# Gated linear attention with a feed-forward: the scaled keys of units 9 to 19 put in token order by VectorE block transposes instead of TensorE transposes

## The chip, the cores and the metric

The kernel runs on one core of one Trainium2 chip, as one launch. The metric is the device time of that launch in microseconds (us): 530.71 us before, the median of three runs (530.29 to 530.88). A core has a matrix engine (TensorE; PE in the profile, with its weight loads listed apart as PEld), a vector engine (VectorE; DVE), a scalar engine (ScalarE; ACT), GpSimd (POOL) and a queue that only issues DMAs (SyncE; SP). Each engine takes its instructions strictly in the order in which they stand in its program and waits on semaphores for the others.

## What is computed

For each of 4 x 8 (batch, head) pairs a 48 x 48 state runs over 768 tokens, decayed row by row by `alpha`; the result `y`, laid out as 3072 tokens of 384 values, goes through a feed-forward network of width 2048 with a leaky ReLU. All in float32.

```python
for t in range(S):                       # S = 768, D = 48
    state = alpha[:, :, t, :, None] * state + einsum('bhd,bhe->bhde', k[:, :, t], v[:, :, t])
    y[:, :, t] = einsum('bhd,bhde->bhe', q[:, :, t], state)
x = y.transpose(0, 2, 1, 3).reshape(B * S, H * D)
h = x @ w_in                             # (3072, 384) @ (384, 2048)
out = maximum(0.01 * h, h) @ w_out
```

## The kernel before

**Units.** The attention is cut into 24 units, `u` = 0 to 23: 6 blocks of 128 tokens times 4 batches, all 8 heads in a unit, two heads stacked on 112 of the 128 partitions (48 rows, a gap of 16, 48 rows) and four such pairs side by side. Units 0 to 19 also carry the state on; the last four (`units[u][0] == NC - 1`) do not. Per unit, `attention` (L455) goes through these steps, with a `yield` behind each:

- `scans` (L308): the decay in feature order, `e`, by a VectorE transpose (from unit 9 on) or by TensorE transposes (before), then cumulative products `pc` and reversed sums `rc`.
- `scaled_q`, `scaled_k` (L334, L342): q times `pc` gives `qs`, k times `rc` gives `ks`, both in feature order. From unit 9 on their transposes are those of L289 on VectorE, out of the loads' buffers.
- `scores` (L350): 8 matmuls of `ks` with `qs`; `mask_scores` (L359) copies and masks them to `sm`.
- `k_tokens` (L375): the scaled keys back in token order. Four TensorE transposes of `ks` into a PSUM bank (L380) and a ScalarE copy into `ktok` (L382).
- `outputs` (L385): `y` from state, queries and masked scores (L395, L401), and `kv` from `ktok` and the values (L412), then `y` into `x` (L418, L419). `next_state` (L421) updates the state.

**Feed-forward.** Three units make a block of 384 tokens, `i` = 0 to 7; its x rows are completed by two small DMAs from SBUF to SBUF (`gather`, L442). For each of 16 slices `f` of the width, `ffn_in` (L484) runs 9 matmuls into `ph` (L493: high and low parts of the weights and of x), then on ScalarE `t` = 0.01 ph (L496), on VectorE `t` = max (L499), on ScalarE `gh` (L501), on VectorE `gl` (L505). `ffn_out` (L510) runs 9 matmuls with `gh` and `gl` into the output banks (L520), three items later (`LAG`). There are two `ph` banks, so the matmuls of item n + 2 need the `t` of item n to be done.

**Stages.** Units 0 to 8 run first. Then blocks 0 and 1 run interleaved, while the weights of the next slices are converted (`converting`, L226: raw words to a high part `hi` and a low part, six VectorE steps up to L265 and two of ScalarE). The first two items of that stage are emitted within the attention of units 7 and 8, by the table `STARTS` (L551), behind the `kt` transposes of L380. From block 2 on, the attention steps of units 9 to 23 are emitted between the items: two steps per item in block 2, one and a half later, eight steps a unit.

**Order.** The code is emitted in this order, and a scheduler then sets the order on each engine when the program is built; `issue_after` (`behind`, L108) holds an instruction behind another. SP issues all loads in its own order, and a load into a used buffer waits there until the buffer's last reader is done.

**Buffers.** q, k and alpha have two load buffers each, and a third one for units 0 to 8; `load_next(u, i)` issues the next load into the buffer that unit u gives up.

Of the kernel before, what the change touches and what calls it, by code (L numbers as in the profile page):

```python
# [22 lines left out]
def gated_linear_attn_ffn(ctx, tc, q, k, v, alpha, w_in, w_out, out):  # L23
    nc = tc.nc
# [3 lines left out]
    P = 128  # L28
    C = 128
    NC = S // C  # L30
    NP = H // 2
# [7 lines left out]
    units = [(t, b) for t in range(NC) for b in range(B)]  # L39
# [18 lines left out]
    AHEAD = 3 * UPB  # L58
# [8 lines left out]
    def bank(tag=None):  # L67
        if tag is None:
            tag = kinds[0]
            kinds.append(kinds.pop(0))  # L70
        return ps_x.tile([P, 512], F32, name=tag)
# [36 lines left out]
    def behind(*key):  # L108

        return tc.issue_after(made[key].ins) if key in made else nullcontext()  # L110

    def places(u, i):
        return loads_sb[i] + [spare[i]] if u < AHEAD else loads_sb[i]

    def loaded(u, i):
        return places(u, i)[u % len(places(u, i))]

    def load_next(u, i):

        for n in range(u + 1, u + 4):  # L120
            if n < NU and n - len(places(n, i)) == u:
                load(n, i)
# [4 lines left out]
    def load(u, i):  # L127
        if u >= NU:
            return
        if u >= AHEAD and later is not None:  # L130
            later.append((load, u, i))
            return
        tb, b = units[u]
        ts = slice(tb * C, (tb + 1) * C)
        t, src = loaded(u, i), (alpha, q, k)[i]
        if u < AHEAD:
            n = H if u or i else H // 2
            for h in range(0, H, n):
                nc.sync.dma_start(
                    by_token(t)[:, h:h + n, 0:D], src[b, h:h + n, ts, :].rearrange("h t d -> t h d")  # L140
                )
            return

        for a in range(4):
            off = 32 * (a % 2)
            nc.sync.dma_start(
                t[32 * a:32 * (a + 1), :].rearrange("j (p r) -> j p r", p=NP)[:, :, 0:RUN - off],
                src[b, a // 2::2, ts, :].rearrange("p (j t) d -> j p (t d)", t=T4)[:, :, off:],
            )

    def load_values(u):
        if u >= NU:
            return
        if u >= AHEAD and later is not None:
            later.append((load_values, u))
            return
        tb, b = units[u]
        made["v", u] = nc.sync.dma_start(
            vals_sb[u % NV].rearrange("t (h d) -> t h d", h=H),
            v[b, :, tb * C:(tb + 1) * C, :].rearrange("h t d -> t h d"),  # L160
        )
# [109 lines left out]
    def banks4():  # L271
        return bank().rearrange("r (p n) -> r p n", p=NP)

    def transposed(u, i, name, **kw):

        src = loaded(u, i)
        if u < AHEAD:
            ps = banks4()
            for p in range(NP):
                last = nc.tensor.transpose(  # L280
                    ps[:, p, :], by_token(src)[:, 2 * p:2 * p + 2, :].rearrange("t h d -> t (h d)"), ident
                )
                if u == 0 and p % 2:
                    with tc.issue_after(last.ins):
                        keep_warm(2)
            return ps
        t = atp.tile([P, NP, C], F32, name=name, **kw)
        src = src.rearrange("r (p n) -> r p n", p=NP)[:, :, 0:RUN]
        nc.vector.transpose(  # L289
            t.rearrange("r p (j t) -> r p t j", t=T4),  # L290
            src.rearrange("r p (t d) -> r p t d", t=T4)[:, :, :, 0:32],
        )
        return t
# [4 lines left out]
    live, masked, sums, dense = {}, {}, {}, {}  # L298
# [35 lines left out]
    def scaled_q(u):  # L334
        pc = live[u][0]
        qT = transposed(u, 1, "qs")
        load_next(u, 1)
        qs = qT if u >= AHEAD else atp.tile([P, NP, C], F32, name="qs")
        nc.vector.tensor_tensor(qs, qT, pc, ALU.mult)
        live[u].append(qs)  # L340
# [9 lines left out]
    def scores(u):  # L350

        pe, qs, ks = live[u]
        ss = [banks4(), banks4()]
        for p in range(NP):
            for s, lo in ((0, 0), (1, HB)):
                nc.tensor.matmul(ss[s][:, p, :], ks[lo:lo + D, p, :], qs[lo:lo + D, p, :], start=True, stop=True)  # L356
        live[u].append(ss)

    def mask_scores(u):  # L359
        ss = live[u].pop()  # L360
        sm = [atp.tile([P, NP, C], F32, name="sm", bufs=3) for _ in (0, 1)]
        for s in (0, 1):
            if s and u >= AHEAD:
                nc.vector.tensor_tensor(sm[s], ss[s], mask.unsqueeze(1).broadcast_to([P, NP, C]), ALU.mult)
                continue
            made["sm", u] = nc.scalar.copy(sm[s], ss[s])  # L366
            made["mask", u] = nc.gpsimd.affine_select(  # L367
                out=sm[s], in_=sm[s], compare_op=ALU.is_ge, fill=0.0, base=0, pattern=[[0, NP], [1, C]], channel_multiplier=-1
            )
        masked[u] = sm  # L370
        with behind("mask", u):
            while scalings:
                nc.gpsimd.tensor_tensor(*scalings.pop(0))  # L373

    def k_tokens(u):  # L375
        if units[u][0] < NC - 1:
            ks = live[u][2]
            kt = bank()
            for p in range(NP):
                made["kt", u] = nc.tensor.transpose(kt[:, p * BR:(p + 1) * BR], ks[0:BR, p, :], ident[0:BR, 0:BR])  # L380
            ktok = atp.tile([P, NP, BR], F32, name="ktok", bufs=1)
            made["sm", u] = nc.scalar.copy(ktok.rearrange("t p d -> t (p d)"), kt[:, 0:NP * BR])  # L382
            live[u][2] = ktok

    def outputs(u):  # L385
        tb, b = units[u]
        i, j = divmod(u, UPB)
        pe, qs, ktok = live[u][:3]
        V, W = vals_sb[u % NV], state[b]
        at = i % 3 * (NG + 1)  # L390
        y = banks4()

        if tb:
            for p in range(NP):
                nc.tensor.matmul(  # L395
                    y[0:BR, p, :], W[0:BR, p, :], qs[0:BR, p, :], start=p == 0, stop=False, skip_group_check=True
                )
        for p in range(NP):
            for s, lo, m in ((0, 0, D if tb else HB), (1, HB, D)):
                c = (2 * p + s) * D  # L400
                nc.tensor.matmul(  # L401
                    y[lo:lo + m, p, :], V[:, c:c + m], masked[u][s][:, p, :],
                    start=not tb and p == 0, stop=p == NP - 1, skip_group_check=True,
                )
        del masked[u]
        kv = None
        if tb < NC - 1:
            kv = bank()[:, 0:NP * D].rearrange("d (p e) -> d p e", p=NP)
            for p in range(NP):
                for s, lo, m in ((0, 0, HB), (1, HB, D)):  # L410
                    h = 2 * p + s
                    made["kv", u] = nc.tensor.matmul(  # L412
                        kv[lo:lo + m, p, :], ktok[:, p, lo:lo + m], V[:, h * D:(h + 1) * D], start=True, stop=True
                    )
        load_values(u + NV)
        live[u] = pe, kv
        xh, xl = (x_sb[0:BR, at:at + NP, n, j * C:(j + 1) * C] for n in (0, 1))
        made["xh", u] = nc.scalar.copy(xh, y[0:BR])  # L418
        made["x", u] = nc.vector.tensor_tensor(xl, y[0:BR], xh.bitcast(F32), ALU.subtract)  # L419
# [35 lines left out]
    def attention(first, last):  # L455

        for u in range(first - 1, last):
            new, old = u + 1 < last, u >= first
            if new:
                scans(u + 1)  # L460
                yield
            if old:
                scores(u)
                yield
                mask_scores(u)
                yield
                k_tokens(u)
                sum_up(u)
                yield
            if new:  # L470
                scaled_q(u + 1)
                yield
                scaled_k(u + 1)
                yield
            if old:
                outputs(u)
                yield
                next_state(u)
                if u % UPB == UPB - 1:
                    gather(u // UPB)  # L480
                    ready.add(u // UPB)
                yield
# [71 lines left out]
    for n, _ in enumerate(st):  # L554
# [7 lines left out]
        u = AHEAD - EARLY + converted  # L562
# [13 lines left out]
    new = coming = None  # L576
    for n in range(len(items) + LAG):
        slices = 0
        if n < len(items):
# [17 lines left out]
            elif i == 0:  # L597
# [3 lines left out]
                old, new, coming = new or iter(()), coming, converting(f + SOON + 1, True)  # L601
# [144 lines left out]
```

## Time and profile before

The profiled execution is one run of its own; its span is what the page's shares and all moments below refer to. It and the median of the timed runs are the same within 0.2 us.

| | before |
|---|---|
| time, median of 3 runs | 530.71 us (530.29 to 530.88) |
| span of the profiled execution | 530.9 us |
| instructions | 9962 |
| mean granted TensorE clock | 0.994 |
| ScalarE busy | 230.7 us (43%) |
| GpSimd busy | 62.6 us (12%) |
| units 0 to 8 | about 0 to 66 us |
| blocks 0 and 1, with the conversion of the weights | about 60 to 164 us |
| blocks 2 to 7, with units 9 to 23 until about 450 us | about 163 to 530 us |

The page's groups are one line each: source line, engine, operation, tile written and tiles read, shape, count, then busy time, mean duration, and the idle time of the engine just ahead of them with what ended it. `a` and `b` are PSUM banks, `small` is the tensor that holds the load buffers, the state and the mask, `large` holds x.

### The profile page before, as it was taken

How to read it: one execution, taken by the hardware profiler on the slowest of the kernel's cores; microseconds unless marked ns; L12 is line 12 of the kernel's file. 1: busy time of each engine (PE TensorE's matmuls, PEld its weight loads, DVE VectorE, ACT ScalarE, POOL GpSimd, SP SyncE). 2: the span in 40 equal slices, each digit the busy share in tenths (PEclk: the TensorE clock that was granted, in tenths of full speed). 3: DMA queues.
4: the chain of work that ended last, by engine and by line, in shares of the span. 5: the costliest groups of instructions: out<-in, count | busy, mean ns of one | idle time of the engine just before them, and what ended most of it. 6: DMA issues, size and time to landing. Idle time of an engine off the chain costs nothing.

```text
span 530.9 us, 9962 instructions
## 1 busy us (share of the span) xinstructions
PE 518.5 (98%) x3778; PEld 500.0 (94%) x3778; DVE 379.0 (71%) x695; ACT 230.7 (43%) x489; POOL 62.6 (12%) x143
## 2 busy tenths in 40 slices
PE   8997999999999999999999999999999999999995
PEld 7886999999999999999999999999999999999995
DVE  6998899999999997777577586585786534333331
ACT  2764855555534444444334444345344444333331
POOL 4554500000000111100101101101010000000000
PEclk9998999999999999999999999999999999999998
DMA  9999975545726533552251431433201000101001
GB/s 144 168 175 170 229 172 133 131 122 141 170 45 184 127 84 81 102 134 49 60 111 30 112 83 44 92 74 86 54 15 25 31 16 1 23 1 44 1 0 51
DMA packets 92982, 46.64 MB, mean 88 GB/s; under 512 B 57856, under 2 KB 90112, under 8 KB 92928
## 3 DMA queue, kind: packets, MB, share of 16 engines
q1 hardware_dynamic: 92928, 45.93, 39.5%
q8 instruction: 32, 0.52, 0.4%
q14 instruction: 22, 0.18, 0.1%
HBM read 38.83 MB, written 4.72 MB: 82 GB/s over the span
## 4 chain that ended last, share of the span: by engine, by line
PE 87%; DVE 7%; DMA 4%; issue 1%; SPq 0%; DVEq 0%; ACT 0%
PE ph L493 35%; PE b L520 32%; PE a L356 4%; PE a L401 3%; PE a L520 3%; DMA small<-in_v_dram 3%; PE a L395 3%; PE a L412 2%; PE b L401 1%; PE a L380 1%; PE b L280 1%; DMA small<-in_alpha_dram 1%; DVE pw L262 1%; DVE gl L505 1%; DVE t L499 1%
## 5 line engine op out<-in xcount | busy, mean ns | idle before, releaser
L493 PE MATMUL ph<-large,w 128*128 128x384 f32 x1152 | 226.6, 338 | 0.5 <-DVE t L499 0.5
L493 PEld LDWEIGHTS ph<-large,w 128*128 128x128 f32 x1152 | 200.1, 188 | 2.8 <-DVE t L499 1.1
L520 PE MATMUL b<-w,gh 128*128 128x384 f32 x672 | 168.9, 340 | 0.0
L499 DVE TENSOR_TENSOR t<-ph,t 128x384 f32<-128x384 f32 x128 | 70.7, 553 | 79.1 <-ACT t L496 78.9
L520 PEld LDWEIGHTS b<-w,gh 128*128 128x128 f32 x672 | 119.4, 188 | 2.1 <-issue 0.4
L496 ACT ACTIVATE t<-ph 128x384 f32<-128x384 f32 x128 | 62.5, 489 | 128.2 <-PE ph L493 128.2
L501 ACT CAST gh<-t 128x384 fp32r<-128x384 f32 x128 | 65.7, 513 | 119.6 <-DVE t L499 119.6
L520 PE MATMUL b<-w,gl 128*128 128x384 f32 x336 | 107.4, 335 | 0.0
L505 DVE TENSOR_TENSOR gl<-t,gh 128x384 fp32r<-128x384 f32 x128 | 70.9, 554 | 34.3 <-ACT gh L501 34.2
L520 PEld LDWEIGHTS b<-w,gl 128*128 128x128 f32 x336 | 62.6, 188 | 0.0
L367 POOL TENSOR_SCALAR_AFFINE_SELECT sm<-sm 128x512 f32<-128x512 f32 x33 | 23.1, 712 | 207.8 <-ACT sm L366 207.8
L356 PEld LDWEIGHTS a<-qs,ks 48*128 48x128 f32 x312 | 24.1, 188 | 5.1 <-issue 4.2
L356 PE MATMUL a<-qs,ks 48*128 48x128 f32 x312 | 28.7, 285 | 0.0
L289 DVE STREAM_TRANSPOSE ks<-small 128x512 f32<-128x512 f32 x15 | 16.7, 1123 | 14.6 <-PE a L380 14.6
L324 POOL COPY pe<-pc 128x4 f32<-128x4 f32 x24 | 4.8, 202 | 163.7 <-DVE pc L314 163.7
L373 POOL TENSOR_TENSOR small<-us,pe 48x192 f32<-48x192 f32 x40 | 22.4, 560 | 1.5
L314 DVE TENSOR_TENSOR_SCAN pc<-e,small 128x128 f32<-128x128 f32 x60 | 20.4, 401 | 0.0
L366 ACT COPY sm<-a 128x512 f32<-128x512 f32 x24 | 14.0, 583 | 14.0 <-PE b L356 12.9
L520 PE MATMUL a<-w,gh 128*128 128x384 f32 x96 | 19.6, 337 | 0.0
L320 DVE TENSOR_TENSOR_SCAN rc<-e,small 128x511 f32<-128x511 f32 x15 | 19.1, 1276 | 0.2
L401 PE MATMUL a<-sm,small 128*48 128x128 f32 x256 | 17.7, 277 | 0.0
L254 ACT CAST w<-bits 128x768 fp32r<-128x768 f32 x16 | 13.4, 838 | 8.4 <-DVE bits L251 7.8
(92 smaller groups left out, 554.4 us busy)
## 6 DMA issues: line engine op xcount, KB each, us to landing
raw<-in_moe_w_out_dram SPq DMA_DIRECT2D x16, 384.0 KB, 3.8
small<-in_v_dram SPq DMA_DIRECT2D x24, 192.0 KB, 3.7
raw<-in_moe_w_in_dram SPq DMA_DIRECT2D x32, 144.0 KB, 4.0
out_dram<-o SPq DMA_DIRECT2D x24, 192.0 KB, 2.0
small<-in_alpha_dram SPq DMA_DIRECT2D x32, 96.0 KB, 2.3
small<-in_q_dram SPq DMA_DIRECT2D x30, 96.0 KB, 2.4
small<-in_k_dram SPq DMA_DIRECT2D x30, 96.0 KB, 2.2
small<-in_alpha_dram SPq DMA_DIRECT2D x30, 80.0 KB, 2.4
```

The costliest lines, as they stand in the source:

```text
L314: nc.vector.tensor_tensor_scan(pc[:, p, :], aT[:, p, :], ones.broadcast_to([P, C]), 1.0, ALU.mult, ALU.mult)
L320: nc.vector.tensor_tensor_scan(flat[2][:, NP * C - 2::-1], flat[0][:, NP * C - 1:0:-1], flat[1][:, NP * C - 2::-1], last, ALU.mult, ALU.add)
L356: nc.tensor.matmul(ss[s][:, p, :], ks[lo:lo + D, p, :], qs[lo:lo + D, p, :], start=True, stop=True)
L367: made["mask", u] = nc.gpsimd.affine_select(out=sm[s], in_=sm[s], compare_op=ALU.is_ge, fill=0.0, base=0, pattern=[[0, NP], [1, C]], chann ...
L373: nc.gpsimd.tensor_tensor(*scalings.pop(0))
L401: nc.tensor.matmul(y[lo:lo + m, p, :], V[:, c:c + m], masked[u][s][:, p, :], start=not tb and p == 0, stop=p == NP - 1, skip_group_check=True,
L493: nc.tensor.matmul(ph, w_in_of(f, wn, g), xt[:, g, :], start=n == 0, stop=n == 3 * NG - 1)
L496: put(ordered, "ACT", lambda: nc.scalar.mul(t, ph, 0.01))
L499: put(ordered, "DVE", lambda: nc.vector.tensor_tensor(t, ph, t, ALU.max))
L501: put(ordered, "ACT", lambda: nc.scalar.copy(gh, t))
L505: made["gl", i, f] = put(ordered, "DVE", lambda: nc.vector.tensor_tensor(gl, t, gh.bitcast(F32), ALU.subtract))
L520: product = nc.tensor.matmul(po[j], gt[:, js], w_out_of(f, wn), start=f == 0 and n == 0, stop=f == NF - 1 and n == 2)
```

## The change

For units 9 to 19 (`turns(u)`) the keys are no longer transposed on TensorE. `turn_keys(u, r)` issues, for each of 4 row blocks r of 32 rows, four VectorE transposes of 32 rows by 4 x 32 columns: sixteen per unit, each turning four 32 x 32 blocks. They write into the buffer of the unit's own q load (`keys_of`), which is free once `scaled_q` has transposed it; `outputs` reads the keys there. So `load_next(u, 1)` moves for these units from `scaled_q` to behind `outputs`. The ScalarE copy to `ktok` and the PSUM bank fall away.

For all units `k_tokens` moves in the code: from ahead of `sum_up` to behind `scaled_q(u + 1)`. For units 0 to 8, whose keys stay on TensorE, the four transposes therefore stand behind the transposes of the next unit's q, and the two kinds of banks change places. At the two points named in `STARTS` the key `("kt", u)` does not exist yet, so the first two items of the feed-forward are emitted there without that hold.

```diff
     def scaled_q(u):
         pc = live[u][0]
         qT = transposed(u, 1, "qs")
-        load_next(u, 1)
+        if not turns(u):
+            load_next(u, 1)
...
+    def turns(u):
+        return u >= AHEAD and units[u][0] < NC - 1
+
+    def keys_of(u):
+        return loaded(u, 1)[:, 0:NP * P].rearrange("t (p e) -> t p e", p=NP)
+
+    def turn_keys(u, r):
+
+        if not turns(u):
+            return
+        Q = 32
+        rs = slice(r * Q, (r + 1) * Q)
+        for c in range(C // Q):
+            cs = slice(c * Q, (c + 1) * Q)
+            nc.vector.transpose(keys_of(u)[cs, :, rs], live[u][2][rs, :, cs])
+
     def k_tokens(u):
-        if units[u][0] < NC - 1:
+        if turns(u):
+            live[u][2] = keys_of(u)
+        elif units[u][0] < NC - 1:
             ks = live[u][2]
...
         load_values(u + NV)
+        if turns(u):
+            load_next(u, 1)
         live[u] = pe, kv
...
             if old:
                 scores(u)
+                turn_keys(u, 0)
                 yield
                 mask_scores(u)
+                turn_keys(u, 1)
                 yield
-                k_tokens(u)
+                turn_keys(u, 2)
                 sum_up(u)
                 yield
             if new:
                 scaled_q(u + 1)
+            if old:
+                turn_keys(u, 3)
+                k_tokens(u)
+            if new:
                 yield
                 scaled_k(u + 1)
                 yield
```

The lines of the changed file are 1 to 27 higher: the turns are L390, the kept TensorE transposes of the keys L399, `ph` matmuls L520, `t` L526, `gl` L532, the matmuls of `y` L414 and L420, of `kv` L431, the masking L365, the gather L470.

VectorE, in block 2, around the masking of unit 10, before:

```order
L364 TENSOR_TENSOR sm<-a,small 128x512
L505 TENSOR_TENSOR gl<-t,gh 128x384
L289 STREAM_TRANSPOSE ks<-small 128x4x4x32
L499 TENSOR_TENSOR t<-ph,t 128x384
L314 SCALAR_TENSOR_TENSOR pc<-e,small 128x128 x4
L315 MEMSET e 128x32
L316 RECIPROCAL small<-pc 128x32
L505 TENSOR_TENSOR gl<-t,gh 128x384
```

And VectorE at the same place in the changed kernel; the L390 rows are the turns of the next unit's keys, 16 in all:

```order
L365 TENSOR_TENSOR sm<-a,small 128x512
L532 TENSOR_TENSOR gl<-t,gh 128x384
L289 STREAM_TRANSPOSE ks<-small 128x4x4x32
L390 STREAM_TRANSPOSE small<-ks 32x4x32 x9
L314 SCALAR_TENSOR_TENSOR pc<-e,small 128x128 x2
L526 TENSOR_TENSOR t<-ph,t 128x384
L314 SCALAR_TENSOR_TENSOR pc<-e,small 128x128 x2
L390 STREAM_TRANSPOSE small<-ks 32x4x32 x6
L526 TENSOR_TENSOR t<-ph,t 128x384
L390 STREAM_TRANSPOSE small<-ks 32x4x32
L315 MEMSET e 128x32
```

The turns stand in runs between the `t` and `gl` steps of the feed-forward; in later units up to 16 stand in one run.

TensorE in unit 6, where the feed-forward begins, in the changed kernel, with what each row waits for; the second `ph` row is the first pair of matmuls of item (1, 0), which reads the x rows of block 1, and `DMAHW1` and `DMAHW2` are the lanes of that block's gather:

```order
L420 MATMUL b<-sm,small 48x128 [waits DMAHW7_49,Pool_49]
L420 MATMUL b<-sm,small 48x128 [waits Pool_49]
L420 MATMUL b<-sm,small 48x128 x6
L520 MATMUL ph<-large,w_667 128x384 [waits DMAHW2_49,DMAHW1_49,DVE_49]
L520 MATMUL ph<-large,w_667 128x384
L431 MATMUL a<-small,ktok 64x48 [waits Activation_49]
```

Before, no `ph` row stands between the `y` and `kv` matmuls of unit 6 and the scores of unit 7; the first one, item (0, 0), stands behind the keys' transposes of unit 7, and item (1, 0) behind those of unit 8:

```order
L401 MATMUL b<-sm,small 48x128 [waits Pool_49]
L401 MATMUL b<-sm,small 48x128 x6
L356 MATMUL a<-qs,ks 128x128 [waits DVE_49]
L356 MATMUL b<-qs,ks 128x128 [waits PE_49]
L356 MATMUL a<-qs,ks 128x128
```

SP, the loads that end with the gather of block 1 (L470), in the changed kernel; the order of these rows before is the same but for q and k of `spare`, which change places:

```order
L139 DMA spare<-in_q_dram 128x8x48 [waits DMAHW4_49,PE_49]
L209 DMA raw<-in_moe_w_in_dram 16x3x128 [waits DMAHW5_49]
L139 DMA spare<-in_k_dram 128x8x48 [waits DMAHW6_49,PE_49]
L158 DMA small<-in_v_dram 128x8x48 [waits DMAHW7_49,PE_49]
L158 DMA small<-in_v_dram 128x8x48 [waits DMAHW0_49,PE_49]
L470 DMA large<-large 16x3x768 [waits DMAHW1_49,DVE_49]
L470 DMA large<-large 16x3x768 [waits DMAHW2_49]
```

So the gather has not moved on SP, while its first reader on TensorE has moved forward by the `kv` matmuls of unit 6 and all of units 7 and 8 up to the scores.

## Prediction

> **What bounds the kernel now.** I read the page's busy shares first, then the chain that ended last:
>
> ```profile
> PE 518.5 (98%) x3778; PEld 500.0 (94%) x3778; DVE 379.0 (71%) x695; ACT 230.7 (43%) x489; POOL 62.6 (12%) x143
> PE 87%; DVE 7%; DMA 4%; issue 1%; SPq 0%; DVEq 0%; ACT 0%
> ```
>
> TensorE ends the kernel, so each stretch taken off it should shorten the whole. But VectorE's 71% is an average. The windows (busy us and instruction counts of PE, PEld, DVE, ACT, POOL, then clock and DMA) show stages:
>
> ```profile
> 110.00:120.00 10.00, 10.00 (x59) 9.89 (x59) 10.00 (x18) 5.78 (x11) 0.00 (x0) 1.00 0.53 148
> 154.10:247.00 92.90, 92.43 (x680) 89.37 (x679) 77.39 (x147) 39.59 (x91) 11.65 (x29) 1.00 0.45 109
> 250.00:400.00 150.00, 150.00 (x1122) 145.71 (x1118) 102.77 (x192) 59.30 (x131) 14.42 (x35) 1.00 0.30 70
> ```
>
> From about 70 to 160 us, where weights are converted, VectorE is as full as TensorE. In 154 to 247, where units 9 onward go twice as densely through block 2, it is busy 77.4 of 92.9 us (15.5 idle); later 102.8 of 150. The change puts its new work first into the stage with little room.
>
> **What is removed.** 44 transposes on TensorE (4 in each of 11 units) and 11 copies on ScalarE. The weight loads around one group:
>
> ```profile
> 203.72 1.57 PEld L493 LDWEIGHTS ph<-large,w 128*128 128x128 f32 x9
> ...
> 205.28 0.50 PEld L380 LDWEIGHTS a<-small,ks 112*128 112x128 f32 x4
> ...
> 205.74 0.30 PEld L520 LDWEIGHTS b<-w,gh 128*128 128x128 f32 x2
> ```
>
> A group holds the stream from 205.28 to 205.74, 0.46 us. I take 0.45 a unit: 5.0 us in all where TensorE is the bound, nothing where VectorE is. The copies (0.54 us each) cost nothing before: ScalarE has 57% idle.
>
> **What a turn costs.** The trace has no transpose of 32 rows. It has those of 512 elements per row, sixteen 32 x 32 blocks per lane against a turn's four:
>
> ```profile
> 161.09 2.04 DVE L289 STREAM_TRANSPOSE ks<-small 128x512 f32<-128x512 f32 x2
> L289 DVE STREAM_TRANSPOSE ks<-small x15: 1101/1133/1137, 161.1 to 404.6; 128x512 f32<-128x512 f32 x15
> 405.54 1.30 DVE L314 TENSOR_TENSOR_SCAN pc<-e,small 128x128 f32<-128x128 f32 x4
> L167 DVE MEMSET small<- 128x128 f32 x6 | 0.9, 165 | 0.0
> L315 DVE MEMSET e<- 128x32 f32 x15 | 1.3, 85 | 0.0
> ```
>
> Two back to back take 2.04 us, one 1.13, so each adds 0.91: a quarter is 0.23. The scans show that short instructions also overlap (four in 1.30 us, about 0.31 each). I add some 0.025 for issue and take **0.255 us** a turn, 4.1 us a unit, 45 us over 11 units. Bounds: 0.31 above (a scan of 128 elements, the slow kind), 0.13 below (a memset of 128 elements, 0.165 with its start-up).
>
> [...]
>
> **What VectorE can take.** In the order on VectorE, from the `e` transpose of unit 9, at 154.13 us before, up to the `t` of block 3's fifth item, stand six units' turns, 96. The rest of that list is what stands in 154.1 to 247.0 of the trace, within a step or two. The matmuls waiting for that `t` began at 247.03:
>
> ```profile
> 154.13 1.10 DVE L289 STREAM_TRANSPOSE e<-small 128x512 f32<-128x512 f32 x1
> ...
> 247.03 1.57 PEld L493 LDWEIGHTS ph<-large,w 128*128 128x128 f32 x9
> L505 DVE TENSOR_TENSOR gl<-t,gh 128x384 fp32r<-128x384 f32 x25 | 13.7, 548 | 4.4 <-ACT gh L501 4.4
> L499 DVE TENSOR_TENSOR t<-ph,t 128x384 f32<-128x384 f32 x24 | 13.2, 549 | 3.1 <-ACT t L496 3.0
> L289 DVE STREAM_TRANSPOSE ks<-small 128x512 f32<-128x512 f32 x7 | 7.7, 1124 | 6.9 <-PE a L380 6.9
> ```
>
> VectorE then needs 77.4 + 96 x 0.255 = 101.9 us. Of the 15.5 idle the 6.9 behind L380 go with the transposes, and most of the waits for ScalarE are filled; I leave 2. So 103.9 where the trace has 92.9: **+11.0 us**, and the 0.45 us of these six units buys nothing. Behind it five units remain, 80 turns or 20.4 us, against 47 us of idle in 250 to 400: they fit, and TensorE gains 5 x 0.45 = **-2.3 us**.
>
> **What the moved `k_tokens` does to the start.** In unit 6 TensorE now meets the first matmuls of item (1, 0) ahead of unit 6's `kv` and unit 7's scores. They need the gather of block 1, which on SP still stands behind two value loads:
>
> ```profile
> 49.92 2.79 SPq L158 DMA_DIRECT2D small<-in_v_dram  x2
> 49.98 0.42 PE L401 MATMUL b<-sm,small 128*48 128x128 f32 x1 [2.79 <-DMA small<-in_v_dram]
> 51.22 1.70 PE L401 MATMUL b<-sm,small 128*48 128x128 f32 x13
> 51.56 0.35 DVE L432 TENSOR_TENSOR us<-us,a 112x192 f32<-112x192 f32 x1 [0.74 <-PE a L412]
> 52.83 1.40 SPq L449 DMA_DIRECT2D large<-large  x2
> ...
> 53.57 0.69 DVE L419 TENSOR_TENSOR large<-b,large 112x512 fp32r<-112x512 f32 x1 [0.79 <-ACT large L418]
> ...
> DMA to landing us min/median/max: 5.1/5.3/5.4
> ```
>
> Issued at 52.83 and 53.5, landing 5.1 to 5.4 us later (the last row, of these two DMAs): about 58.9. TensorE ended `y` of unit 6 soon after 51.2, so it would stand some 7 us. Queued behind are `kv` of unit 6 (done by 51.6 before), the scores of unit 7 (52.85 before) and the next q transposes. VectorE has `y` of unit 6 (53.57 to 54.26) and then stands at `us` of unit 6 until about 60, 5.7 us. Both engines are near full from there on:
>
> ```profile
> sum 25.00, PE 25.00 PEld 23.58 DVE 22.30 ACT 15.81 POOL 7.29; mean PE 2.78 PEld 2.62 DVE 2.48 ACT 1.76 POOL 0.81
> 152.79 0.96 DVE L265 TENSOR_TENSOR w<-pw,bits 128x768 fp32r<-128x768 f32 x1
> 154.77 1.23 PEld L493 LDWEIGHTS ph<-large,w 128*128 128x128 f32 x7
> ```
>
> The first row sums 50 to 75 us: 1.4 us idle on the weight loads, 2.7 on VectorE. The others show VectorE ending the last low weights at 153.75, 1 us ahead of the matmuls that use them. So little is caught up: of 5.7 I keep **+5.0 us**, between 0 (the gather lands in time) and 7.
>
> **Edits at nothing.** The q load is issued a unit's length later, behind `outputs`; its data are wanted a whole unit after that, and its DMAs land fast:
>
> ```profile
> small<-in_q_dram SPq DMA_DIRECT2D x30, 96.0 KB, 2.4
> ```
>
> A unit lasts 16 us or more in these stages, so some 14 us cover it; what stands behind it on SP (values, `alpha`, outputs) has the same lead. If that cover were gone, each q load would add up to 2.4 us, 26 in all. One PSUM bank less per unit only loosens things. In units 0 to 8 the keys' transposes now follow q's; VectorE is over 90% busy there, and I count nothing, within 1 us.
>
> **Sum.** 530.9 (the profiled span; the median of the runs, 530.71, is the same within 0.2) + 5.0 + 11.0 - 2.3 = 544.6; I say **544**.
>
> **Rivals.**
> - *The gather is no wait.* If the values of unit 6, and so the queue behind them, land 7 us earlier in the new order, only VectorE's load remains: 530.9 + 11.0 - 2.3 = 539.6. For it: only SP's order was compared, not its moments. Against: those rows have kept their places.
> - *Cheap turns.* The transposes in the trace write with a stride of four elements, the turns write rows of 32; if the stride is what costs, a turn goes at the memset's pace: 0.165 us with start-up, about 0.16 back to back at most. Then 77.4 + 96 x 0.16 + 2 = 94.8: +1.9, and 530.9 + 5.0 + 1.9 - 2.3 = 535.5. Against it: the memset of L315 writes 32 elements 16 apart in 85 ns, no slower for its stride. [...]
> - *Runs of turns also stop the later units.* 16 turns in one run hold `t` for 4.1 us. The next `ph` but one starts 4.7 us after a `ph` ends (three groups of 1.57), of which `t` needs about 1.2; 3.5 us of delay pass unseen, the rest stalls, with the masking and the scan behind it by 1 to 1.5 us in the five later units: 544.6 + 7 = 551.
> - *Faster: VectorE's gaps take all turns.* Place: 154 to 247 us. Price: TensorE's 5.0 us, 526 if the gather does not wait either. It decides from 0.14 us a turn down (77.4 + 96 x 0.14 + 2 is the stage's length); with the gather's wait it comes out at 531, no faster.
> - That the change doesn't do what it says is excluded: the order has 11 x 16 turns, and no TensorE transposes of keys from unit 9 on.
>
> **Chances.** Forecast 0.50, no wait for the gather 0.18, cheap turns 0.14, later stalls too 0.09, faster 0.09. The range has to hold the forecast's own bounds (0.20 to 0.31 us a turn is -5 to +5; the gather's wait -5 to +2) and the two milder rivals: 532 to 553. A measurement of this kernel tells about 0.2% (1 us) from no change: faster 0.09, the same 0.05 (cheap turns with little waiting), slower 0.86.
>
> **What would show it.** A turn's group in the lines: 16 x 11, VectorE's pitch of 0.25 in the timeline. In the stretch that was 154 to 247, VectorE near 100% busy, `ph` matmuls idle with `t` (L526) named as releaser. At 51 to 59 us, TensorE idle ahead of L520, released by the DMA `large<-large`, and VectorE idle at `us`. In 250 to 400, no new idle on TensorE. Wrong, if turns back to back take 0.16 us or less, if TensorE shows no wait for the gather, or if most of the new idle time lies behind 260 us.

## The result and the profile after

The changed kernel takes **565.13 us**, the median of four runs (562.7 to 565.41), beside 530.8 us for the kernel before, also of four runs (530.29 to 531.85): a ratio of 1.0636, with a 95% interval of 1.0611 to 1.066. That is slower by 34.3 us, in the direction of the forecast, but 12 us beyond the upper end of its range. The profiled execution has a span of 563.4 us, 32.5 above that of before, and a mean TensorE clock of 0.972 (0.994 before). A span is 1.7 us shorter than the time of its run (563.4 beside 565.07). By that, as an estimate, the profile of before, at 530.9, belongs to a run of some 532.5 us, 1.8 above the median, and is not the same as the median within 0.2. So the span grew by 1.8 us less than the time.

Of the page of the changed kernel, first the busy shares and the chain that ended last, by engine and by line:

```profile
PE 529.4 (94%) x3734; PEld 506.5 (90%) x3734; DVE 431.7 (77%) x871; ACT 222.7 (40%) x478; POOL 65.0 (12%) x143
PE 51%; DVE 32%; DMA 7%; SPq 4%; issue 4%; ACT 1%; POOL 0%; DVEq 0%; ACTq 0%
PE ph L520 21%; PE b L547 19%; DVE small L390 8%; DVE gl L532 3%; DVE t L526 3%; SPq L146 3%; DVE pc L314 2%; DMA small<-in_q_dram 2%; PE a L357 2%; DVE qs L289 2%; PE a L420 2%; PE a L547 2%; DVE ks L289 2%; PE a L414 2%; DVE pw L262 2%
```

Before, the chain ran over TensorE for 87% of the span and over VectorE for 7%. Now it is 51% and 32%, and the third line names what came in: the turns (L390), and the q load (its issue on SP, L146, and its DMA). The groups say which waits are new: the matmuls of `ph` stand 17.4 us, 9.3 of them for the gather, and the q transposes of VectorE stand 11.3 us for their load, where they stood for nothing before.

```profile
L520 PE MATMUL ph<-large,w 128*128 128x384 f32 x1152 | 232.4, 344 | 17.4 <-DMA large<-large 9.3
L390 DVE STREAM_TRANSPOSE small<-ks 32x128 f32<-32x128 f32 x176 | 53.4, 304 | 2.5
L289 DVE STREAM_TRANSPOSE qs<-small 128x512 f32<-128x512 f32 x15 | 16.5, 1103 | 11.3 <-DMA small<-in_q_dram 11.3
```

Where the 32.5 us arise is read from the same instruction in both timelines. The first mark is the `e` transpose of unit 9, the second the matmuls of the item that waits for the `t` of block 3's fifth item (247.03 before), the prediction's own two ends of the stage around block 2. In the changed kernel:

```profile
163.16 1.11 DVE L289 STREAM_TRANSPOSE e<-small 128x512 f32<-128x512 f32 x1
...
278.40 1.51 PEld L520 LDWEIGHTS ph<-large,w 128*128 128x128 f32 x9
```

| stretch | before | after | difference | predicted |
|---|---|---|---|---|
| start to `e` of unit 9 | 154.13 | 163.16 | +9.0 | +5.0 |
| from there to the second mark | 92.90 | 115.24 | +22.3 | +11.0 |
| from there to the end of the span | 283.9 | 285.0 | +1.1 | -2.3 |

All three terms were too small, and the largest error is in the middle one. The start is understated here: in the runs whose first units are those of before (e1, e3 to e7, e10, e11), `e` of unit 9 starts between 152.1 and 153.3, 0.8 to 2.0 us ahead of the profile of before. The windows of that stretch and of the next (columns as in the prediction):

```profile
163.16:278.40 115.24, 103.38 (x668) 98.21 (x667) 109.34 (x245) 36.69 (x86) 14.29 (x29) 0.91 0.34 83
278.40:430.00 151.60, 149.28 (x1099) 143.34 (x1098) 127.31 (x274) 54.57 (x127) 16.79 (x35) 1.00 0.31 73
```

VectorE is busy 109.34 of 115.24 us (77.39 of 92.90 before), and TensorE, which stood there for 0.5 us (92.90 less 92.43), now stands for 11.9: the stage is VectorE's now, as forecast, only longer.

**The start.** The timeline of the changed kernel in unit 6 (start, duration, engine, line, idle time ahead and its releaser), and the windows there:

```profile
47.69 1.08 PE L420 MATMUL b<-sm,small 128*48 128x128 f32 x16
...
51.68 1.59 SPq L470 DMA_DIRECT2D large<-large  x2
...
58.05 0.98 PE L520 MATMUL ph<-large,w 128*128 128x384 f32 x2 [9.28 <-DMA large<-large]
...
60.17 0.36 DVE L453 TENSOR_TENSOR us<-us,a 112x192 f32<-112x192 f32 x1 [8.42 <-PE a L431]
```

```profile
50.00:55.00 5.00, 0.00 (x0) 0.00 (x0) 1.75 (x3) 0.88 (x1) 0.76 (x1) 0.85 1.39 168
55.00:60.00 5.00, 1.95 (x20) 1.45 (x20) 0.00 (x0) 0.00 (x0) 0.00 (x0) 0.50 1.04 224
60.00:65.00 5.00, 5.00 (x31) 4.78 (x31) 3.92 (x7) 2.61 (x7) 2.52 (x4) 0.63 1.03 249
```

This is the forecast wait, at the forecast place, with the forecast releasers, but 9.28 us long on TensorE (7 predicted) and 8.42 on VectorE (5.7). The gather landed at 58.05, 0.85 us earlier than predicted; what I had wrong is the other end. The prediction let `y` of unit 6 end at about 51.9, where its own row (51.22, 1.70 us long) ends at 52.9; in the new order `y` is done at 48.8, 4.1 us earlier than that, so TensorE reached the wait sooner. And it comes out of it at half clock (0.50, then 0.63).

### The profile page after: what moved, and what is told of

It is laid out like the page before. It is cut to its first block, busy times and chain, and to the rows that moved or that the text cites. A ratio compares the mean times of both kernels' runs of the same rounds, so it can differ in the third digit from the quotient of the medians.

```text
span 563.4 us, 10027 instructions
## 1 busy us (share of the span) xinstructions
PE 529.4 (94%) x3734; PEld 506.5 (90%) x3734; DVE 431.7 (77%) x871; ACT 222.7 (40%) x478; POOL 65.0 (12%) x143
## 4 chain that ended last, share of the span: by engine, by line
PE 51%; DVE 32%; DMA 7%; SPq 4%; issue 4%; ACT 1%; POOL 0%; DVEq 0%; ACTq 0%
PE ph L520 21%; PE b L547 19%; DVE small L390 8%; DVE gl L532 3%; DVE t L526 3%; SPq L146 3%; DVE pc L314 2%; DMA small<-in_q_dram 2%; PE a L357 2%; DVE qs L289 2%; PE a L420 2%; PE a L547 2%; DVE ks L289 2%; PE a L414 2%; DVE pw L262 2%
## 5 line engine op out<-in xcount | busy, mean ns | idle before, releaser
L520 PE MATMUL ph<-large,w 128*128 128x384 f32 x1152 | 232.4, 344 | 17.4 <-DMA large<-large 9.3
L520 PEld LDWEIGHTS ph<-large,w 128*128 128x128 f32 x1152 | 204.0, 192 | 21.5 <-issue 9.9
L547 PE MATMUL b<-w,gh 128*128 128x384 f32 x672 | 171.7, 344 | 0.0
L547 PEld LDWEIGHTS b<-w,gh 128*128 128x128 f32 x672 | 122.7, 192 | 2.8 <-ACT gh L528 0.6
L526 DVE TENSOR_TENSOR t<-ph,t 128x384 f32<-128x384 f32 x128 | 70.4, 550 | 52.3 <-ACT t L523 51.8
L532 DVE TENSOR_TENSOR gl<-t,gh 128x384 fp32r<-128x384 f32 x128 | 71.3, 558 | 31.2 <-ACT gh L528 31.0
L390 DVE STREAM_TRANSPOSE small<-ks 32x128 f32<-32x128 f32 x176 | 53.4, 304 | 2.5
L368 POOL TENSOR_SCALAR_AFFINE_SELECT sm<-sm 128x512 f32<-128x512 f32 x33 | 21.4, 660 | 187.3 <-ACT sm L367 187.3
L357 PE MATMUL a<-qs,ks 48*128 48x128 f32 x312 | 30.9, 289 | 0.0
L357 PEld LDWEIGHTS a<-qs,ks 48*128 48x128 f32 x312 | 25.9, 191 | 4.8 <-issue 3.7
L324 POOL COPY pe<-pc 128x4 f32<-128x4 f32 x24 | 6.4, 268 | 190.9 <-DVE pc L314 190.9
L289 DVE STREAM_TRANSPOSE qs<-small 128x512 f32<-128x512 f32 x15 | 16.5, 1103 | 11.3 <-DMA small<-in_q_dram 11.3
L367 ACT COPY sm<-a 128x512 f32<-128x512 f32 x24 | 14.0, 585 | 24.7 <-PE b L357 22.3
L420 PE MATMUL a<-sm,small 128*48 128x128 f32 x256 | 18.5, 278 | 0.3 <-DVE sm L365 0.3
```

Of the source, the lines that this page charges most:

```text
L289: nc.vector.transpose(t.rearrange("r p (j t) -> r p t j", t=T4), src.rearrange("r p (t d) -> r p t d", t=T4)[:, :, :, 0:32],)
L390: nc.vector.transpose(keys_of(u)[cs, :, rs], live[u][2][rs, :, cs])
L420: nc.tensor.matmul(y[lo:lo + m, p, :], V[:, c:c + m], masked[u][s][:, p, :], start=not tb and p == 0, stop=p == NP - 1, skip_group_check=True,
L520: nc.tensor.matmul(ph, w_in_of(f, wn, g), xt[:, g, :], start=n == 0, stop=n == 3 * NG - 1)
L526: put(ordered, "DVE", lambda: nc.vector.tensor_tensor(t, ph, t, ALU.max))
L532: made["gl", i, f] = put(ordered, "DVE", lambda: nc.vector.tensor_tensor(gl, t, gh.bitcast(F32), ALU.subtract))
```

## The experiments

Times below are compared by ratios to the kernel before in the same comparison, times 531 us where a difference in us is given. The rows of an experiment have its own line numbers: `ph` matmuls L520 to L529, turns L390 to L397, `t` L526 to L535.

**e1, the old place of `k_tokens` for the units that keep TensorE.**

```diff
                 turn_keys(u, 2)
+                if not turns(u):
+                    k_tokens(u)
                 sum_up(u)
...
                 turn_keys(u, 3)
-                k_tokens(u)
+                if turns(u):
+                    k_tokens(u)
```

> Undoes the moved k_tokens alone: units 0 to 8 call k_tokens where they did before, and the turns stay. Theory A (the start costs what the e transpose of unit 9 shows, 163.16 against 154.13 us, and nothing of it is caught up later): e of unit 9 back at about 154, the time 565.1 - 9.0 = about 556. Rival B (block 2 is bound by VectorE, so a late start is caught up behind it, and the loss is that of the turns alone): 562 or more. Under both the wait of TensorE for the gather in unit 6 is gone.

554.3 us, ratio 1.0438 (1.0417 to 1.0459). That is 0.0198 below the change, 10.5 us; the `e` of unit 9 starts at 153.23. The wait for the gather is gone from the group of the `ph` matmuls, and what is left of it is all for `t`:

```profile
L523 PE MATMUL ph<-large,w 128*128 128x384 f32 x1152 | 229.4, 341 | 11.4 <-DVE t L529 11.4
```

Theory A; nothing of the start is caught up.

**e2, that move alone** (`turns` returns False for every unit).

```diff
     def turns(u):
-        return u >= AHEAD and units[u][0] < NC - 1
+        return False
```

> The moved k_tokens alone: no turns, q load in its old place, all keys on TensorE. Theory A (the start costs 9.0 us and stays): 530.7 + 9.0 = about 540, with the 9.3 us wait for large<-large in unit 6. Rival B (the 2.6 us of idle time that VectorE has in units 7 and 8 and its 15.5 us in block 2 take the delay up): 534 or less.

541.56 us, ratio 1.0199 (1.0178 to 1.0219): +10.6 us with no turn in the kernel.

```profile
L520 PE MATMUL ph<-large,w 128*128 128x384 f32 x1152 | 228.0, 339 | 10.8 <-DMA large<-large 10.3 <-DVE t L526 0.5
```

Taken out of the change or put into the kernel before, the move is worth the same, and nearly all the `ph` waiting is for the gather.

**e9, only the hold of the first two items taken from the kernel before**, with `k_tokens` where it was.

```diff
-            with behind(*STARTS[n]):
+            with nullcontext():
                 gs[len(gs)] = ffn_in(i, f)
```

> The kernel before with one thing taken away: the hold of the first two feed-forward items behind the kt transposes. k_tokens stays where it was. Theory A (the loss at the start is that of the matmuls of item (1, 0), which now stand ahead of unit 7's scores and wait for the gather; the order of the transposes costs nothing): as e2, 531 + 10 = about 541. Rival B (the changed order of the keys' and the queries' transposes in units 0 to 8 is what costs): within 1 us of before.

540.62 us, ratio 1.0173 (1.0113 to 1.0233), +9.2 us, with 7.8 us of waiting for `large<-large`. So the lost hold is the cause of nearly all of it. The exchange of the two kinds of transposes may cost the 1.4 us between e9 and e2, but that is inside e9's interval and not clear of nothing.

**e3, the turned keys in a buffer of their own**, on top of e1: that of `ktok`, with the 48 rows of each head packed side by side so that it fits.

```diff
-        if not turns(u):
-            load_next(u, 1)
+        load_next(u, 1)
...
     def keys_of(u, at=0, n=2 * D):
-        return loaded(u, 1)[:, 0:NP * P].rearrange("t (p e) -> t p e", p=NP)
+        if u not in turned:
+            turned[u] = atp.tile([P, NP, BR], F32, name="ktok", bufs=1).rearrange("t p d -> t (p d)")
...
-        if turns(u):
-            load_next(u, 1)
```

> As e1, and the turned keys go to a buffer of their own (that of ktok, packed to 96 columns a pair), so the q load is issued in scaled_q as before. Theory A (the q loads issued late cost VectorE the 11.3 us of idle time put down to small<-in_q_dram, 10.2 of them before 400 us, and about 6 of these reach the end): e1 less 6, about 550, and no wait of the qs transposes for DMA. Rival B (VectorE is full in these stretches whatever the loads do): within 1.5 us of e1. What is left over 530.7 is then the price of the turns themselves.

548.51 us, ratio 1.0329 (1.0309 to 1.035), 5.8 us below e1. The waits of the q transposes are gone (this row had 11.9 in e1), and the turns themselves cost the same 303 ns:

```profile
L289 DVE STREAM_TRANSPOSE qs<-small 128x512 f32<-128x512 f32 x15 | 16.4, 1095 | 0.0
...
L396 DVE STREAM_TRANSPOSE ktok<-ks 32x128 f32<-32x128 f32 x176 | 53.3, 303 | 5.5
```

The size is that of theory A. But e3 changes two things, the room and the place of the load in the code. (It also turns the row blocks in another order, and `kv` of these units takes 48 key columns for every head, where one head of each pair had 64.)

**e10, the own buffer, with the q load still written behind `outputs`.**

```diff
-        load_next(u, 1)
+        if not turns(u):
+            load_next(u, 1)
...
         load_values(u + NV)
+        if turns(u):
+            load_next(u, 1)
```

> As e3 (keys in a buffer of their own), but with the q load of units 9 to 19 issued behind outputs, as in the change. Theory A (the moment of the q load is what cost the 5.8 us between e1 and e3): as e1, about 554, with some 11 us of waits for small<-in_q_dram. Rival B (the room is what cost: in e1 the turns share a buffer with the q load and its readers, and stand elsewhere in VectorE's order): as e3, 548.5.

548.55 us, ratio 1.0323 (1.0293 to 1.0353), the same as e3: theory A falls. The place in the code is worth nothing; the shared room is worth 5.8 us, and with the own buffer no q transpose waits for its load, wherever the call stands. The place where most of the 5.8 us arises is the q transpose of unit 14. First the changed kernel:

```profile
254.12 0.61 PE L431 MATMUL a<-small 128*64 128x48 f32 x16
255.01 1.08 DVE L289 STREAM_TRANSPOSE e<-small 128x512 f32<-128x512 f32 x1
256.12 1.74 SPq L146 DMA_DIRECT2D small<-in_alpha_dram  x4
257.95 1.80 SPq L146 DMA_DIRECT2D small<-in_q_dram  x4
261.77 1.10 DVE L289 STREAM_TRANSPOSE qs<-small 128x512 f32<-128x512 f32 x1 [2.32 <-DMA small<-in_q_dram]
263.76 4.74 DVE L390 STREAM_TRANSPOSE small<-ks 32x128 f32<-32x128 f32 x15
269.15 2.61 PE L520 MATMUL ph<-large,w 128*128 128x384 f32 x7 [2.86 <-DVE t L526]
```

and e10, the load for the same transpose, and the transpose:

```profile
205.94 1.80 SPq L146 DMA_DIRECT2D small<-in_q_dram  x4
...
243.00 1.09 DVE L289 STREAM_TRANSPOSE qs<-small 128x512 f32<-128x512 f32 x1
```

With the keys in the load buffer, the load for unit 14 has to wait until `kv` of unit 12 has read them (254.12 to 254.73). On SP it stands behind the alpha load, which waits for the `e` transpose (255.01 to 256.09). So it is issued at 257.95, and VectorE stands 2.32 us for it. Then come fifteen turns ahead of a `t`, and the `ph` matmuls stand 2.86 us behind that `t`. With a buffer of its own, the same call gives a load that waits only for the q transpose of unit 12, and it goes out 37 us ahead of its use.

That the waiting alone makes the 5.8 us is not shown. Between the two marks of the stage e1 takes 113.1 us and e3 107.7, but VectorE waits for the q load only 2.1 us of that in e1. The room also changes the order: e1 has 96 turns ahead of the second mark, as the change has, e3 and e10 have 80. Item for item, the `ph` matmuls of e1 are 0.4 us behind those of e3 just ahead of unit 14's turns (251.58 and 251.22) and 5.0 us behind after them (258.96 and 253.94). There e1 has both the late load and fifteen turns in one run ahead of a `t`; e3 has no wait and eleven turns, those of unit 13, and its turns of unit 14 come at 268 to 275 us. No run has one without the other.

**e4, turns in units 15 to 19 only**, on top of e3 (`return u >= 15 and units[u][0] < NC - 1`).

> As e3, with turns in units 15 to 19 only (80 turns, all behind block 2; units 9 to 14 keep the TensorE transposes). Theory A (the prediction's term: the turns fit into VectorE's idle time there and TensorE gains 0.45 us a unit): 530.7 - 2.3 = 528.4. Rival B (16 turns in one run, 5.0 us at 0.31 each, hold t and stop TensorE for about 1.5 us a unit, and each stop is followed by a lowered clock): 530.7 - 2.3 + 7.5 = 536 or more.

533.17 us, ratio 1.005 (1.0029 to 1.0071): +2.7 us, between the two theories, on the side of B. A run of fourteen turns ahead of a `t` passes unseen once, and stops TensorE another time, at 355 to 365 us, with the clock down afterwards. Beside the trace of before, the `ph` matmuls of e4's profiled run gain 1.6 us from 278 to 355 us, as theory A has it, and lose 3.8 from there to 370:

```profile
315.85 4.65 DVE L396 STREAM_TRANSPOSE ktok<-ks 32x128 f32<-32x128 f32 x14
320.53 0.56 DVE L534 TENSOR_TENSOR t<-ph,t 128x384 f32<-128x384 f32 x1
```

```profile
315.00:320.00 5.00, 5.00 (x39) 4.63 (x38) 4.56 (x15) 0.15 (x1) 0.00 (x0) 1.00 0.37 78
...
360.00:365.00 5.00, 3.13 (x13) 3.13 (x14) 4.23 (x12) 2.07 (x6) 0.00 (x0) 0.83 0.20 73
365.00:370.00 5.00, 5.00 (x26) 5.00 (x26) 4.84 (x11) 3.32 (x10) 2.09 (x5) 0.83 0.39 113
```

**e5, the same with each group of four turns held behind the newest `gl`.**

```diff
-            nc.vector.transpose(keys_of(u, (0, 32, 48, 80)[r], Q)[cs], live[u][2][rs, :, cs])
+            with behind("now"):
+                nc.vector.transpose(keys_of(u, (0, 32, 48, 80)[r], Q)[cs], live[u][2][rs, :, cs])
...
-        made["gl", i, f] = put(
+        made["now",] = made["gl", i, f] = put(
```

> As e4, but each group of four turns is held behind the gl of the newest feed-forward item, so that no run on VectorE is longer than 8 turns (2.5 us) where e4 has runs of 10 to 16. Theory A (what e4 lost is the one stop of TensorE behind a long run at 355 to 365 us and the low clock after it; the transposes taken from TensorE are worth 0.45 us a unit): TensorE idle for t below 0.5 us, 531.2 - 2.3 = about 529. Rival B (the turns cost the later units something wherever they stand): 532 or more, as e4.

531.51 us, ratio 1.0009 (0.9993 to 1.0026): no difference from before that can be measured. The stops of `ph` are gone (0.5 us, as before), but new small ones stand at the matmuls of `kv`, which now wait for the last turns:

```profile
L438 PE MATMUL a<-small,ktok 128*48 128x48 f32 (+1 forms) x304 | 13.2, 216 | 1.0 <-DVE ktok L397 0.9
```

So theory A holds for the long runs (e5 is 2.2 us below e4) and not for the gain: 2.3 us were expected, and none shows. The time lies nearer to that of rival B. The waits of `kv` are 0.9 us of what is missing; the rest stays open.

**e11, turns in units 9 to 14 only**, on top of e3 (`return AHEAD <= u < 15`).

> As e3 with turns in units 9 to 14 only (96 turns, all in the stage around block 2). Theory A (that stage is bound by VectorE, and units 15 to 19 cost 2 us, as e4 says): 548.5 - 2.0 = about 546.5. Rival B (the later units share the loss, by work that the stage pushes into them): 541 or less.

545.42 us, ratio 1.0264 (1.0234 to 1.0293), +14.0 us; e3 is 3.5 above it. Theory A within 1.1 us: most of the turns' price is paid around block 2, and the later units add some 3.

**e6 and e7, half of the turns left out, and all of them**, on top of e3, with one `ktok` buffer kept from unit 8 on.

```diff
-        for c in range(C // Q):
+        for c in range(0, C // Q, 2):
```

In e7 the loop runs over nothing (`for c in ():`).

> As e3 with half of the turns left out (eight of sixteen a unit, in every unit 9 to 19, so half of the turned keys stay stale). Theory A (VectorE's room in block 2 decides): 48 turns there make 77.4 + 48 x 0.31 = 92.3 us plus some 2 idle, hardly more than the 92.9 of before: 528 to 533. Rival B (each turn costs the same, by the delay it brings to t): halfway between e7 and e3, about 537.

> As e3 with all turns left out: units 9 to 19 use the keys of unit 8, so the keys cost neither TensorE nor VectorE nor ScalarE anything. It measures the gain on the other side. Theory A (TensorE ends the kernel and each unit's four transposes hold it for 0.45 us): 531.2 - 5.0 = about 526. Rival B (the stream closes up only in part, since the next matmuls wait for t anyway): 529 or more.

e7 takes 525.34 us, ratio 0.9899 (0.9876 to 0.9923): the TensorE transposes are worth 5.4 us in all, theory A. e6 takes 531.84 us, ratio 1.0021 (1.0008 to 1.0033), the time of theory A. The first eight turns of a unit cost 6.5 us together, the other eight 16.4 (e3 less e6). So the price is not the same for each turn; it fits a stage whose room is used up by the later ones. Theory A's account of the stage was too kind, though. Between the two marks e6 takes 97.32 us, 4.4 more than before, with only 40 turns ahead of the second mark and VectorE busy 91.42 us; from there to the end it is some 4 us shorter (279.9 against 283.9), which makes the time come out:

```profile
152.57:249.89 97.32, 93.23 (x662) 88.11 (x661) 91.42 (x187) 35.31 (x84) 13.46 (x29) 1.00 0.41 105
```

**e8 and e12, the price of a turn by itself**: the kernel before with extra transposes late in the program. The forms of e8, `rows[r]` being 32 rows and `wide` a load buffer as 4 x 128:

```python
nc.vector.transpose(wide[1][rows[n % 4], :, rows[n // 4]], wide[0][rows[n // 4], :, rows[n % 4]])  # L625
nc.vector.transpose(wide[1][rows[n % 4], :, rows[n // 4]], wide[0][rows[n % 4], :, rows[n // 4]])  # L627
nc.vector.transpose(wide[1][:, :, rows[n // 4]], wide[0][:, :, rows[n // 4]])                      # L629
nc.vector.transpose(dst[rows[n % 4], 0:32], src[rows[n % 4], 0:32])                                # L631
nc.vector.transpose(dst[rows[n % 4], 0:256], src[rows[n % 4], 0:256])                              # L633
nc.vector.transpose(dst, src)                                                                      # L635
```

> The kernel before with extra VectorE instructions on load buffers no longer used, late, where VectorE has room: a turn (32 rows to another 32 rows, 4 blocks), the same within its own 32 rows, the same on all 128 rows, one block (32x32), eight blocks (32x256), sixteen on 128 rows (128x512), a copy of 32x128. Theory A (a fixed part that back to back does not hide, and a price per block of 32 columns; from 0.91 for sixteen and 0.31 for four: 0.05 a block and 0.11 fixed): 32x32 at 0.16, 32x256 at 0.51, and the turn 0.31 whether or not it changes rows or has 128 rows. Rival B (the change of rows or the strided tile costs): a turn within its own rows, or on 128 rows, at 0.25 or less.

The groups of e8:

```profile
L635 DVE STREAM_TRANSPOSE small<-small 128x512 f32<-128x512 f32 x12 | 8.4, 704 | 0.1
L633 DVE STREAM_TRANSPOSE small<-small 32x256 f32<-32x256 f32 x12 | 5.2, 437 | 0.3
L627 DVE STREAM_TRANSPOSE small<-small 32x128 f32<-32x128 f32 x12 | 3.7, 304 | 0.4
L625 DVE STREAM_TRANSPOSE small<-small 32x128 f32<-32x128 f32 x12 | 3.6, 303 | 0.3
L629 DVE STREAM_TRANSPOSE small<-small 128x128 f32<-128x128 f32 x12 | 3.1, 284 | 0.0
L631 DVE STREAM_TRANSPOSE small<-small 32x32 f32<-32x32 f32 x12 | 2.4, 203 | 0.3
```

The form of theory A holds and rival B falls (the turn within its own rows takes the same 304 ns; on 128 rows it is 284, not 250 or less), but the numbers are others: from 32 to 512 elements the duration rises from 203 to 704 ns, which is, as an estimate, 1.04 ns an element, with 0.17 us left at no element. A plain copy of 32 x 128 takes 220 ns (L637 of e8). Sixteen blocks take 0.70, not the 1.12 us of L289 in the kernel, from which I had scaled. e12 asks why, with L289's strides put in one by one:

```diff
+    gaps = gaps.rearrange("r p (t d) -> r p t d", t=T4)[:, :, :, 0:32]
+    even = src.rearrange("r (p t d) -> r p t d", p=NP, t=T4)
+    flat = dst.rearrange("r (p t j) -> r p t j", p=NP, t=T4)
+    wove = dst.rearrange("r (p j t) -> r p t j", p=NP, t=T4)
...
+    # eight each: flat<-even L636, wove<-even L638, flat<-gaps L640, wove<-gaps L642
+    # then 32x128 with the same rows each time L644, and 128x128 L646
```

> The kernel before with extra VectorE transposes of 512 elements on 128 rows, late, in six groups of eight: plain rows read and plain rows written; plain read and written with the stride of 4 elements that the L289 transposes have; read across the gaps of the load buffers and written plain; both, which is L289's own form; then the turn with the same rows each time; then four blocks on 128 rows. Theory A (one element per cycle and a fixed part, and the stride of the writes is what makes L289 take 1.12 us): 0.70, 1.12, 0.70, 1.12. Rival B (the reads across the gaps cost): 0.70, 0.70, 1.12, 1.12. The turn with the same rows: 0.30 long and 0.31 to 0.33 apart under theory A of e8; overlapped (under 0.27 apart) if the change of rows from one turn to the next is what keeps them apart.

The groups of e12, and one run of each of the two small forms:

```profile
L638 DVE STREAM_TRANSPOSE small<-small 128x512 f32<-128x512 f32 x8 | 8.9, 1107 | 0.0
L642 DVE STREAM_TRANSPOSE small<-small 128x512 f32<-128x512 f32 x8 | 8.7, 1088 | 0.1
L640 DVE STREAM_TRANSPOSE small<-small 128x512 f32<-128x512 f32 x8 | 5.7, 706 | 0.1
L636 DVE STREAM_TRANSPOSE small<-small 128x512 f32<-128x512 f32 x8 | 5.6, 703 | 0.1
```

```profile
443.19 1.29 DVE L644 STREAM_TRANSPOSE small<-small 32x128 f32<-32x128 f32 x4
444.42 1.03 DVE L646 STREAM_TRANSPOSE small<-small 128x128 f32<-128x128 f32 x5
```

Theory A, as to the stride: writing four elements apart costs 0.4 us per 512 elements (1107 ns against 703), reading across the gaps nothing (706 against 703). A cycle of VectorE, of which the theory speaks, is not shown; what is measured is the 1.04 ns an element of e8. Four blocks on 128 rows follow one another at (1.03 - 0.26) / 4 = 0.19 us, each 0.26 long, so these overlap; the turns with the same rows are 0.33 apart and do not. That last comparison decides nothing on the change of rows: each of those turns also waited by a semaphore for the one before, since they wrote the same place.

## Why the prediction was wrong, step by step

**What bounds it, and the direction: right.** VectorE becomes the bound around block 2 (busy 109.3 of 115.2 us), TensorE waits for the gather in unit 6 (9.28 us), and the TensorE transposes are worth what was said (e7: 5.4 us, 5.0 predicted). The sum failed in four terms. What the prediction had, and what the runs showed in its place:

| term | predicted | measured | by |
|---|---|---|---|
| the start | +5.0 | +9.2 to +10.6 | the change less e1; e2; e9 |
| the lent q buffer (its load "at nothing") | 0 | +5.8 | e1 less e3, and e10 |
| turns in units 9 to 14, less TensorE's gain there | +11.0 | +14.0 | e11 |
| turns in units 15 to 19, less the gain | -2.3 | +2.7 to +3.5 | e4; e3 less e11 |

With 10.5, 5.8, 14.0 and 3.5 the terms are steps of one chain of runs (the change, e1, e3, e11, before), so they add up to the whole, 33.8 us, by themselves. The check is that two of them come out alike when they are put into the kernel before alone: the start (10.6 in e2, 9.2 in e9) and the later units (2.7 in e4).

**The start** was mis-sized. "Of 5.7 I keep +5.0" took TensorE's arrival from the old trace, where unit 6 was held up by other things (among them 2.79 us for its values), and 1 us early at that. And the argument that little is caught up was sound; it should have been followed to its end: the whole wait, with the half clock behind it, stays.

**The price of a turn** was mis-sized, 0.255 for 0.317 us. Sixteen turns in a row take 5.07 us in the changed kernel:

```profile
309.03 5.07 DVE L390 STREAM_TRANSPOSE small<-ks 32x128 f32<-32x128 f32 x16
```

Two steps of the working failed, in opposite directions. A quarter of 0.91 us was taken for the cost of the elements; e8 and e12 show that those 0.91 hold the price of a strided write, which the turns do not pay (the prediction's rival of cheap turns was right about the stride, and the argument against it, from a short memset, was wrong; but the price it put in, 0.16 us, was further off than the forecast's). And the start-up was put at 0.025, since short instructions overlap; by e8 (203 ns at 32 elements, 704 at 512) 0.17 us are left at no element, and the turns do not overlap: the sixteen above take 0.317 us each, at a mean of 0.304 long. Four blocks on 128 rows do overlap (e12, 0.19 apart, 0.26 long). Why the turns do not, no run shows. The lower bound of 0.13 stands in no row: the nine memsets of 128 elements (L167), 0.165 long, start 0.14 apart, from 1.49 to 2.61 us in the trace of before.

**The stage** of the changed kernel can be set beside the prediction's own sum. Its 103.9 us were 77.4 of other work, 24.5 of turns and 2 idle. The trace has 29.1 of turns (96 of 303 ns, +4.6), 80.2 of other work (109.3 - 29.1, +2.8, of which one `e` transpose and one product with `rc` more ahead of the mark are 1.5) and 5.9 idle (+3.9, of which 2.3 is the q load): 115.2. In e3, without the lent buffer, 80 turns stand ahead of the mark and the stage takes 107.7.

**The q load, put "at nothing",** is the step that failed in kind. "Some 14 us cover it" counted the cover from the place of the call in the code, which is worth nothing (e10). What decides is the last reader of the buffer. The change made `kv`, on another engine and itself late, the reader, and on SP the load then stood behind another that waits: at unit 14 it is issued 3.8 us ahead of its transpose, in e10 37 us. The value taken was 0, and lending the buffer cost 5.8. The bound, 26 us "if that cover were gone", held. How much of the 5.8 is waiting for the load, and how much the order of the turns that comes with the shared room, stays open.

**The later units** failed in sign. In "they fit" the sum of idle time was right and beside the point: 37 of the 47 us of idle lay in gaps behind ScalarE's `t` and `gh`, and in the two orders tried the turns held up a `t` (e4) or a `kv` (e5). The rival that runs of turns also stop the later units had the mechanism; its price of 7 us compares with the 5.0 between -2.3 and +2.7.

**Of the signs it named**, those at the start and in the stage came as described. "In 250 to 400, no new idle on TensorE" did not hold: 2.3 us in the window from 278.40 to 430 (151.60 less 149.28), where before it stood for nothing.

## What to carry to other kernels

Moved work is priced where it lands: read how much room that engine has in that stage; here the first half of the turns cost 6.5 us and the second 16.4. A buffer that is lent out gets a new last reader, and here its next load moved behind that reader and behind what SP held at that point (issued 3.8 us ahead of its use at unit 14, where the own buffer had 37); how far ahead of its use the load was issued before is the number to check. A hold that hangs on a name which a moved step no longer sets disappears without a word: here this alone cost 9.2 to 10.6 us, and no version of the change that was tried beats the kernel before.

## What the runs showed of the hardware

- A VectorE transpose with plain rows took 203 ns at 32 elements a row, 303 at 128, 437 at 256 and 704 at 512 (e8, 32 rows, at 512 elements 128; as an estimate from these, 0.17 us and 1.04 ns an element), and one of 512 elements 0.4 us more when it wrote four elements apart (e12: 1107 ns against 703); no other stride was run. The transposes of L289 in this kernel write four elements apart as well, at 1.10 us each.
- After some stops TensorE went on at a granted clock of 0.50. In the changed kernel the same nine matmuls took 1.72 us at 226.91, and 3.25 behind the 3.49 us stop ahead of `kv`; the granted clock was 0.50 in 235 to 240 us and 0.88 in the next 5. Behind the stop of 2.86 us that ends at 269.15 it was 0.50 in 270 to 275 and 0.97 in the next 5, and seven matmuls took 2.61 us. Not every stop did it: in e1, behind one of 3.29 us, seven matmuls took 1.48 us, and the page's clock digit for 249 to 263 us is 9 (0.9 or more). What decides is not shown. Two rows of the changed kernel, and one of e1:

```profile
226.91 1.72 PE L520 MATMUL ph<-large,w 128*128 128x384 f32 x9
...
235.90 3.25 PE L520 MATMUL ph<-large,w 128*128 128x384 f32 x9
```

```profile
258.96 1.48 PE L523 MATMUL ph<-large,w 128*128 128x384 f32 x7 [3.29 <-DVE t L529]
```

  At the start the change stands 9.3 us for the gather and loses 10.5. What the half clock costs in the stage that VectorE bounds, no run isolates.
